# Squaring q and k one quad later in a fused attention and mixture-of-experts kernel

## The chip, the cores and the metric

The kernel runs on one core of a Trainium2 chip. The time is the device time of one execution in microseconds (us). Each run is classed fast or slow (slow for a single core: over 1.5% above the fastest run of the same kernel), and ratios use fast runs alone. PE is TensorE, ACT ScalarE, DVE VectorE, POOL GpSimd, SP the queue that issues most transfers. L189 is line 189 of the kernel.

## The reference

Attention over 8 batches and 12 heads (448 tokens, head size 64) with RMS-normalised q and k, then a soft mixture of 8 experts with 32 slots.

```python
q_n, k_n = rmsnorm(q, g_q), rmsnorm(k, g_k)         # x / sqrt(mean(x*x) + 1e-6) * g
attn = softmax(q_n @ k_n.T / 8)
x = (attn @ v) as [3584, 768]
logits = x @ phi                                    # 768 x 32
slot_input = softmax_over_tokens(logits).T @ x
slot_out[e] = relu(slot_input[e] @ w1[e]) @ w2[e]   # 8 experts, 768x1024 and 1024x768
out = softmax_over_slots(logits) @ slot_out
```

## The kernel before

A *quad* is four heads; there are 24 quads, three per batch. Iteration Q of the loop computes scores, exponentials and products of quad Q, in seven score steps, and prepares later quads between them. The preparation of one quad is: load q and k (f32, 448 KB each), square them (ACT for q, POOL for k), sum the squares (DVE), two activations for the reciprocal root (ACT), scale to bf16 (POOL), transpose (PE), copy out (DVE). v is loaded by four transfers and copied to bf16 on POOL. Every third iteration (4, 7, 10, ...) also carries the expert work of one batch: `moe_logits` after step 1 and `moe_sin` after step 5; its last products spill into the iteration behind it. The expert weights (16 of 1.5 MB in bf16, cast by the transfer from f32) are loaded by POOL during the loop, three of them by way of a copy in DRAM.

```python
place("raw", 2 * 2 * 2 * NT * D, 3)     # q and k as loaded: three quads
place("sq", 2 * 2 * 2 * NT * D, 1)      # their squares: one
place("qkn", 2 * NT * 128, 2)           # scaled q and k: two
place("vraw", 2 * 2 * NT * D, 2)
# ...
for Q in range(NQ + 2):
    # load(Q + 4): q and k, on the SP queue       (special cases for Q == 0 left out)
    # score(Q, 0); square(Q + 3, 0) on ACT; square(Q + 3, 1) on POOL; products of Q - 1
    # score(Q, 1); rowsum(Q + 3, 0)
    # score(Q, 2); trans(Q + 1, 0); evac(Q + 1, 0); scaleqk(Q + 2, 0)
    # score(Q, 3); norm(Q - 1, 1); trans(Q + 1, 1); vcopy(Q + 1); scaleqk(Q + 2, 1); loadv(Q + 3)
    # score(Q, 4); ov(Q, 0, 0, 4); evac(Q + 1, 1)
    # score(Q, 5); ov(Q, 0, 4, 7); rowsum(Q + 3, 1)
    # score(Q, 6); norm(Q, 0); rsqrt(Q + 3); loads of expert weights
```

Each engine, and the SP queue, works through its instructions in this order. `norm` (DVE) frees the PSUM that the next `ov` (PE) writes.

The softmax here doesn't subtract the row's maximum and nothing guards it: scores larger than these inputs give would overflow.

## Time and profile before

| | before |
|---|---|
| median of the first three runs | 331.62 us (328.18 to 333.1) |
| span of the profiled run | 329.2 us |
| first exponential of iteration 1 / of iteration 21 | 30.1 / 239.2 us |
| after the last exponential | 67.4 us |
| ACT, POOL, PE, DVE busy | 59, 50, 71, 58% |

The start of an iteration is read from the first of its seven exponentials (L252 on ACT). An iteration without any stall takes 7.62 us here; the mean is 10.46.

### The profile page before, as it was taken

How to read it: one execution, taken by the hardware profiler on the slowest of the kernel's cores; microseconds unless marked ns; L12 is line 12 of the kernel's file. 1: busy time of each engine (PE TensorE's matmuls, PEld its weight loads, DVE VectorE, ACT ScalarE, POOL GpSimd, SP SyncE). 2: the span in 40 equal slices, each digit the busy share in tenths (PEclk: the TensorE clock that was granted, in tenths of full speed). 3: DMA queues.
4: the chain of work that ended last, by engine and by line, in shares of the span. 5: the costliest groups of instructions: out<-in, count | busy, mean ns of one | idle time of the engine just before them, and what ended most of it. 6: DMA issues, size and time to landing. Idle time of an engine off the chain costs nothing.

```text
span 329.2 us, 8387 instructions
## 1 busy us (share of the span) xinstructions
PE 234.6 (71%) x3564; PEld 167.0 (51%) x3564; DVE 192.0 (58%) x315; ACT 193.6 (59%) x268; POOL 164.4 (50%) x187
## 2 busy tenths in 40 slices
PE   8465988578878675719788576847688768889910
PEld 3233666356556454417565354635465558874400
DVE  5644787578686485726977485745756551126820
ACT  4385897579767683737787576753797600006710
POOL 0375987659497295619688196637693000000000
PEclk9757899699998799987999799789799975555555
DMA  6967999996979939994999959999999997006996
GB/s 214 244 157 229 226 258 265 243 257 144 257 218 208 279 75 246 238 288 114 239 252 187 249 147 242 242 261 263 216 188 207 212 370 271 4 4 249 401 415 277
DMA packets 45350, 74.53 MB, mean 226 GB/s; under 512 B 3968, under 2 KB 36736, under 8 KB 44928
## 3 DMA queue, kind: packets, MB, share of 16 engines
q1 hardware_dynamic: 29616, 48.77, 47.1%
q0 software_dynamic: 15376, 25.22, 43.2%
q8 instruction: 28, 0.46, 0.6%
q14 instruction: 10, 0.08, 0.1%
q10 hardware_dynamic: 320, 0.00, 0.1%
HBM read 88.18 MB, written 15.73 MB: 316 GB/s over the span
## 4 chain that ended last, share of the span: by engine, by line
DMA 31%; PE 30%; DVE 11%; ACT 10%; POOL 8%; issue 4%; SPq 2%; ACTq 0%; POOLq 0%
DMA arena<-in_q_dram 22%; PE ov L265 7%; PE sc L251 7%; ACT arena L252 6%; DMA arena<-in_k_dram 6%; POOL arena L207 4%; DVE eT L319 3%; PE hTp L472 3%; PE soTp L481 3%; PE op L511 3%; DVE arena L276 3%; PE qkTp L225 2%; ACT arena L189 2%; DMA g<-in_g_q_dram 2%; POOL arena L187 2%
## 5 line engine op out<-in xcount | busy, mean ns | idle before, releaser
L252 ACT ACTIVATE arena<-sc 128x896 bf16<-128x896 f32 x168 | 147.4, 914 | 31.8 <-PE sc L251 31.1
L251 PE MATMUL sc<-arena 128*128 128x448 bf16 x336 | 101.6, 388 | 39.1 <-ACT arena L252 38.4
L265 PEld LDWEIGHTS <-arena 128*128 128x128 bf16 x1344 | 64.9, 104 | 63.3 <-DVE arena L276 32.2
L265 PE MATMUL ov<-arena 128*128 128x65 bf16 (+1 forms) x1344 | 72.6, 207 | 27.8 <-DVE arena L276 27.7
L195 DVE TENSOR_REDUCE ss<-arena 128x14 f32<-128x896 f32 x48 | 52.0, 1085 | 67.7 <-ACT arena L189 59.9
L207 POOL TENSOR_TENSOR arena<-arena,rs 128x896 bf16<-128x896 f32 x47 | 80.5, 1713 | 13.1 <-ACT rs L200 6.9
L187 POOL TENSOR_TENSOR arena<-arena 128x896 f32<-128x896 f32 x21 | 35.3, 1682 | 67.4 <-DMA arena<-in_k_dram 27.5
L251 PEld LDWEIGHTS <-arena 128*128 128x128 bf16 x336 | 26.7, 104 | 43.7 <-issue 41.7
L189 ACT ACTIVATE arena<-arena 128x896 f32<-128x896 f32 x27 | 25.5, 945 | 37.3 <-DMA arena<-in_q_dram 35.3
L225 PE MATMUL qkTp<-ident,arena 128*128 128x128 bf16 x360 | 32.6, 241 | 2.2 <-DVE arena L207 1.1
L276 DVE TENSOR_TENSOR arena<-ov,rd 128x512 bf16<-128x512 f32 x48 | 33.2, 691 | 1.7
L515 ACT ACTIVATE wown<-op,arena 128x768 f32<-128x768 f32 x14 | 12.4, 899 | 35.9 <-PE op L512 35.9
L225 PEld LDWEIGHTS <-arena 128*128 128x128 bf16 x360 | 26.2, 109 | 9.7 <-POOL arena L207 3.2
L236 DVE COPY arena<-qkTp 64x896 bf16<-64x896 bf16 x48 | 29.6, 617 | 1.3 <-PE qkTp L225 0.4
L232 DVE TENSOR_SCALAR arena<-qkTp,gg 128x896 bf16<-128x896 bf16 x24 | 16.2, 676 | 8.3 <-PE qkTp L225 8.2
L511 PE MATMUL op<-arena,eT 32*128 32x512 bf16 x28 | 16.0, 618 | 1.4 <-ACT wown L515 0.7
L517 DVE TENSOR_SCALAR wown<-op,arena 128x768 f32<-128x768 f32 x14 | 14.2, 1017 | 4.6 <-PE op L512 4.4
L290 DVE COPY arena<-xTp 128x1024 bf16<-128x1024 bf16 x24 | 16.3, 680 | 0.7 <-PE xTp L287 0.7
L287 PE MATMUL xTp<-ident,arena 128*128 128x128 bf16 x192 | 14.6, 219 | 1.4 <-DVE arena L276 1.0
L287 PEld LDWEIGHTS <-arena 128*128 128x128 bf16 x192 | 12.7, 98 | 5.9 <-DVE arena L276 1.2
L319 DVE COPY eT<-eTp 32x448 bf16<-32x448 bf16 x8 | 15.2, 1901 | 0.2
L275 DVE RECIPROCAL rd<-ov 128x8 f32<-128x8 f32 x48 | 9.9, 207 | 6.0 <-PE ov L265 5.5
(63 smaller groups left out, 195.6 us busy)
## 6 DMA issues: line engine op xcount, KB each, us to landing
wown<-in_moe_w_dram POOLq DMA_DIRECT2D x10, 1536.0 KB, 15.5
arena<-in_q_dram SPq DMA_DIRECT2D x24, 448.0 KB, 9.1
arena<-in_k_dram SPq DMA_DIRECT2D x24, 448.0 KB, 10.6
out_dram<-wown SPq DMA_DIRECT2D x12, 768.0 KB, 8.9
arena<-in_v_dram SPq DMA_DIRECT2D x48, 128.0 KB, 7.0
arena<-in_v_dram SPq DMA_DIRECT2D x48, 96.0 KB, 6.4
scr<-in_moe_w_dram POOLq DMA_DIRECT2D x3, 1536.0 KB, 16.2
arena<-in_moe_w_dram POOLq DMA_DIRECT2D x3, 1536.0 KB, 13.2
```

Source lines behind the costliest of these rows:

```text
L187: nc.gpsimd.tensor_tensor(sq(t), r, r, op=MUL)
L189: nc.scalar.activation(out=sq(t), in_=r, func=ACTF.Square)
L195: nc.vector.reduce_sum(sss[Q][:, t], sq(t).rearrange("p (r d) -> p r d", d=D), axis=AX)
L207: (eng or nc.gpsimd).tensor_tensor(qkn(Q, t).rearrange("p s (r d) -> p s r d", r=2), raw(Q)[:, t].rearrange("p r (s d) -> p s r d", d=D), ...
L225: nc.tensor.transpose(pts[t][:, i], qkn(Q, t)[:, s], ident)
L236: nc.vector.tensor_copy(kT(Q)[r, :, hh].rearrange("p w (s c) -> p w s c", s=NT), pt[r, :, 1 - hh:8 - hh])
L251: nc.tensor.matmul(sc[:, j, :S], kT(Q)[:, w].rearrange("p h c -> p (h c)")[:, kc:kc + 128], qT(Q)[:, w], start=True, stop=True)
L252: nc.scalar.activation(out=at("attn", i).rearrange("p (h c) -> p h c", h=2), in_=sc[:, :, :S], func=ACTF.Exp, scale=0.125)
L265: nc.tensor.matmul(ovs[w][:, c, o0:o0 + n], attn(i)[:, C0[c]:C0[c] + 128], mov, start=(first and i == lo and c % 2 == 0), stop=(i in (6, 13)),
L276: nc.vector.tensor_tensor(xq(Q).rearrange("p c (h w d) -> p c h w d", h=2, w=2)[:, :, :, w], o[:, :, :, :D], rd.to_broadcast([128, 4, 2, D ...
L287: nc.tensor.transpose(xps[Q][:, i], xq(Q)[:, i % 4, i // 4 * 128:i // 4 * 128 + 128], ident)
L511: nc.tensor.matmul(op[:, 0], eTtok(j, s), so4[r, :512], start=True, stop=True, tile_position=tp)
```

## The change

The intent: square quad Q+2 in iteration Q instead of Q+3, and scale it in the second half of the same iteration. A raw buffer is then held for a shorter time, and with three of them q and k of two further quads can be under way. One buffer of scaled q and k has to do. The core of the diff (prologue, first iteration and index shifts cut):

```diff
-    place("qkn", 2 * NT * 128, 2)
+    place("qkn", 2 * NT * 128, 1)
...
+    loadw(0)
...
-            square(Q + 3, 0)
-            square(Q + 3, 1, True)
+        if ahead:
+            square(Q + 2, 0)
+            square(Q + 2, 1, True)
...
-            rowsum(Q + 3, 0)
+        if ahead:
+            rowsum(Q + 2, 0)
...
-        if Q + 2 < NQ:
-            scaleqk(Q + 2, 0)
+        if ahead:
+            rowsum(Q + 2, 1)
...
             trans(Q + 1, 1)
             vcopy(Q + 1)
-        if Q + 2 < NQ:
+        if ahead:
+            rsqrt(Q + 2)
+            scaleqk(Q + 2, 0)
             scaleqk(Q + 2, 1)
...
-        while wnext < NPRE and Q >= wnext * 9 // 5:
+        while wnext < NPRE and Q >= (wnext * 5 + 2) // 3 - 1:
             loadw(wnext)
             wnext += 1
-        if Q in (NQ - 7, NQ - 6, NQ - 5):
-            castw(2 * E - NSCR + Q - (NQ - 7))
+        if Q in (NQ - 9, NQ - 7, NQ - 5):
+            castw(2 * E - NSCR + (Q - (NQ - 9)) // 2)
```

Besides the intent, the sum over the squares of k stands ahead of `norm(Q - 1, 1)` on DVE; the weights go out at other iterations.

More of the change, by code (lines that the diff above doesn't have):

```diff
@@ L338 @@
     rsqrt(1)
-    vcopy(0)
     for t in range(2):
         scaleqk(1, t)
-    wnext = 0
+    vcopy(0)
+    loadw(0)
+    wnext = 1
     for Q in range(NQ + 2):
-        on, ahead = Q < NQ, Q + 3 < NQ
+        on, ahead = Q < NQ, Q + 2 < NQ
         moe = Q - 2 if 0 <= Q - 2 < NQ else None
         mb = moe // QB if moe is not None and moe % QB == QB - 1 else None
-        if Q + 4 < NQ or Q == 0:
-            for q4 in ((3, 4) if Q == 0 else (Q + 4,)):
-                if q4 == 3 or Q > 0:
-                    load(q4, 0)
-                    load(q4, 1)
+        for q4 in (3, 4) if Q == 0 else (Q + 4,):
+            if q4 < NQ:
+                load(q4, 0)
+                load(q4, 1)
         if on:
             score(Q, 0)
-        if Q == 0:
-            square(2, 0)
-            rowsum(2, 0)
-        elif ahead:
-            square(Q + 3, 0)
-            square(Q + 3, 1, True)
+        if ahead:
+            square(Q + 2, 0)
+            square(Q + 2, 1, True)
         if 0 <= Q - 1 < NQ:
@@ L370 @@
             ov(Q - 1, 1, 10, 12)
-        if Q == 0:
-            square(2, 1)
-            rowsum(2, 1)
-            rsqrt(2)
-        elif ahead:
-            rowsum(Q + 3, 0)
+        if ahead:
+            rowsum(Q + 2, 0)
         if mb is not None:
@@ L396 @@
             vcopy(Q + 1)
-        if Q + 2 < NQ:
+        if ahead:
+            rsqrt(Q + 2)
+            scaleqk(Q + 2, 0)
             scaleqk(Q + 2, 1)
-        if Q + 3 < NQ:
-            loadv(Q + 3) if Q else (loadv(2), loadv(3))
+        for q3 in (2, 3) if Q == 0 else (Q + 3,):
+            if q3 < NQ:
+                loadv(q3)
         if on:
@@ L406 @@
             evac(Q + 1, 1)
-        if Q == 0:
-            load(4, 0)
-            load(4, 1)
-            square(3, 0)
-            square(3, 1, True)
-            rowsum(3, 0)
         if on:
@@ L416 @@
             ov(Q, 0, 4, 7)
-        if ahead:
-            rowsum(Q + 3, 1)
         if mb is not None:
@@ L426 @@
             moe_x(Q - 1)
-        if ahead:
-            rsqrt(Q + 3)
         if Q == 1:
             nc.gpsimd.dma_start(out=phi_s, in_=moe_phi.rearrange("(dc dp) s -> dp dc s", dp=128))
-        while wnext < NPRE and Q >= wnext * 9 // 5:
+        while wnext < NPRE and Q >= (wnext * 5 + 2) // 3 - 1:
             loadw(wnext)
             wnext += 1
-        if Q in (NQ - 7, NQ - 6, NQ - 5):
-            castw(2 * E - NSCR + Q - (NQ - 7))
+        if Q in (NQ - 9, NQ - 7, NQ - 5):
+            castw(2 * E - NSCR + (Q - (NQ - 9)) // 2)
         if Q in (NQ - 4, NQ - 3, NQ - 2):
```

## The prediction

> **What bounds the kernel now.** I read the page's table of slices first. The attention loop fills slices 2 to 31 (8.2 us each); behind it come the expert layers and the output.
>
> ```profile
> ACT  4385897579767683737787576753797600006710
> POOL 0375987659497295619688196637693000000000
> DMA  6967999996979939994999959999999997006996
> ```
>
> No compute engine stays at 9 through the loop: ScalarE and GpSimd jump between 1 and 9. The DMA row is at 9 in most slices but has holes (3, 4, 5, 6, 7). So the loop alternates between waiting for transfers and leaving the transfers idle. The chain that ended last says the same:
>
> ```profile
> DMA 31%; PE 30%; DVE 11%; ACT 10%; POOL 8%; issue 4%; SPq 2%; ACTq 0%; POOLq 0%
> ```
>
> Next the list of waits, for whom ScalarE and GpSimd (the squares, L189 and L187) wait, and for whom the load queue waits:
>
> ```profile
> ACT arena L189 <- DMA arena<-in_q_dram: 35.3, 11, 6.7
> POOL arena L187 <- DMA arena<-in_k_dram: 27.5, 6, 6.7
> ```
>
> ```profile
> SPq L129 <- POOL arena L217: 134.7, 21, 10.3
> ```
>
> The squares wait 35.3 us for q in 11 places. The queue waits for GpSimd's copies of v before it issues the next v, and behind those v, in order, stand the next q and k. One case, from the chain between 47 and 61 us:
>
> ```profile
> 47.32 0.81 ACT arena L252
> 48.13 0.44 ACT arena L189
> 48.57 11.08 DMA arena<-in_q_dram
> ...
> 59.67 0.95 ACT arena L189
> 60.62 0.81 ACT arena L252
> ```
>
> q of quad 7 is issued at 48.57, 1.2 us into iteration 3 (first exponential 47.3), and is wanted as soon as the first exponential of iteration 4 is through, at about 55.7. It has 7.2 us and takes 11.08: a 3.92 us stall. Of three raw buffers one is squared now, one waits squared for its scaling, so only one load can be under way, for less than an iteration.
>
> Taking every seventh exponential as the start of an iteration, iteration 1 starts at 30.1 us, iteration 21 at 239.2: 10.46 us each. Undisturbed ones (2, 3, 6, 15) take 7.62; 21 to 23, without new q or k, take 22.5 together. The tail after the last exponential (261.7 to 329.2) is 67.5 us.
>
> **What the Trainium skill says.** "DMA: Bandwidth & Descriptors", section "Issuing engines are not separate DMA queues": transfers issued by any engine share the same 16 DMA engines and interleave. The trace agrees: in 8 us windows without expert weights, q/k/v move 170 to 206 GB/s without filling the engines (shares 0.61 and 0.73); beside a weight load, at shares of 1.10 to 1.13, they get only 118 GB/s and the weights 138. "Perfetto Trace Analysis", section "Optimization Strategy": a gap that repeats on the engine that should be saturated can mean too few buffers for the next tile. That is the pattern here, and the SBUF is given: three raw buffers stay, only their use changes. Same page, "What "DMA-bound" means": find which DMA resource binds before calling a kernel DMA-bound. I do that by the windows below.
>
> **The change part by part.**
>
> *Squares one quad later.* Iteration Q squares Q+2 instead of Q+3 and scales Q+2 in the same iteration. No instruction's work is removed: 24 times the same two squares, sums and scalings. What moves is the deadline. The buffer of q(Q+4) comes free, as before, when Q+1 is scaled near the end of iteration Q-1, but it is wanted at the start of Q+2 instead of Q+1. Its allowance grows from about 7.2 to about 7.2+7.6-1 = 14 us (the 1 us since scaling ends a little later), while the median landing is 9.1 us for q, 10.6 for k and the longest q 17.1. Most stalls of one transfer should go.
>
> *What the transfers then allow.* Not all 35 us come back, because the 16 engines have a rate. From the page:
>
> ```profile
> q1 hardware_dynamic: 29616, 48.77, 47.1%
> q0 software_dynamic: 15376, 25.22, 43.2%
> ```
>
> q0 (weights) takes 0.432*329.2/25.22 = 5.64 us of all engines per MB; q1 0.471*329.2/48.77 = 3.18, and in windows with q/k/v alone 3.4. Until iteration 21 the loop needs 24*1.376 = 33.0 MB of q/k/v and 13 weight loads of 1.573 = 20.4 MB: 33.0*3.4 + 20.4*5.64 = 227 us of share. The share saturates above 1, as two windows show (columns after the five engines: PE clock, DMA share, GB/s):
>
> ```profile
> 54.80:69.40 14.60, 10.30 (x149) 7.75 (x150) 7.58 (x12) 7.64 (x12) 10.00 (x12) 0.77 1.10 263
> 116.80:126.30 9.50, 8.01 (x149) 6.13 (x150) 8.07 (x12) 7.61 (x12) 9.20 (x14) 1.00 0.66 119
> ```
>
> At 1.13, 227/1.13 = 201 us is an estimate of the floor, so iteration 21 could not start before about 203 us; it starts at 239.2 now. The difference, 36 us, is holes such as the second window (0.66 of 1.13 in 9.5 us is 4 us lost). The floor is about (203-27)/20 = 8.8 us per iteration.
>
> *One buffer of scaled q/k.* Scaling Q+2 must now follow the transposes of Q+1 in the same iteration. They are issued after the third and fourth score; scaling comes after the fourth exponential anyway. I charge nothing.
>
> *A tighter compute cycle.* Square of k, sum, the two rsqrt activations and two scalings now lie in one chain through GpSimd: 1.68 + 1.09 + 0.6 + 2*1.71 = 6.8 us, plus some 0.2 of hand-over, plus 0.94 when a weight load is issued: 7.0 to 7.9 us. Above 7.62 in about 13 of 24 iterations by some 0.3: 4 us, largely under the transfer floor.
>
> *Start.* Iteration 0 lasts 13.6 us now, with squares of both quads 2 and 3, and ends on the sum and rsqrt of quad 3. It loses quad 3's share; loads of quads 3 and 4 are issued at about 20 instead of 27 to 29 us, the first weights at about 21 instead of 28.3, into slices where the DMA row shows 7 and 9. Iteration 1 should start near 27: 3 us gained.
>
> *Weights.* The three casts to scratch and the loads go out slightly earlier in iterations; bytes are equal. The tail should stay at 67.5 us.
>
> Sum: iteration 1 at 27; twenty iterations at 9.1 (floor 8.8 with a little lost, since compute at 7.6 to 7.9 is not far below and jitter costs) = 182; last three 22.5; tail 67.5: 299 us of span. The timed run lies 1.8 above its span (330.95 against 329.2), and I add 2 for what I overlook: 303 us.
>
> **Rivals.** (1) *The transfers are already full*: the row shows 9 nearly everywhere, and depth brings nothing but longer landings. For it: saturated windows at 1.10 and more carry the worst stalls. Against it: about 24 us of holes by share in iterations 1 to 20, and 6 more in iteration 0. If only half of the holes close: 316 us. (2) *The new chain through GpSimd binds.* For it: late k now holds up rsqrt, in order on ScalarE after the fourth exponential, and the sum on VectorE ahead of a normalisation that frees the PSUM of the next products. If it makes 9.8 us of each iteration, 20*0.7 = 14 us more than my sum: 317. (3) *Everything hides*: stalls vanish, compute at 7.9 binds and the floor is lower than estimated; 20*1.2 = 24 us less: 279. It contradicts the share count, so I give it little. (4) *The tail pays*: the last weights (three loads at 7.4 us each, from 212 GB/s alone) land late after a shorter loop. They are issued in iterations 20 to 22, as before, and wanted five expert pairs later; against it.
>
> **Range and chances.** Between half of the holes closed (316) and a perfect floor (294). Faster by over 2% means below 325; it needs only 7 of some 30 us of holes. Faster 0.95, within 2% 0.04, slower 0.01.
>
> **What would show it.** The squares' waits for q and k should fall from 35.3 and 27.5 us to under 15 each; the DMA row should lose most of its 3s to 7s, with shares of 1.05 to 1.13 through iterations 1 to 20; median landing of q and k should rise (to about 12 to 15 us) as two quads queue; iterations should even out near 9 us instead of 7.6 to 16; the tail stays within 2 us of 67.5. I am wrong if the waits fall but the iterations stay above 10 us (rival 2: rsqrt waiting for sums, GpSimd or VectorE on the chain), if holes remain in the DMA row, or if the tail grows by what the loop gains.

## The result, and the profile after

The changed kernel took 307.31 us (median of four runs, 302.56 to 308.82), the kernel before 332.36 beside it. A ratio here is the mean of one kernel's fast runs over that of the other's of the same rounds, so not quite the ratio of the medians: 0.9206, with a 95% interval of 0.898 to 0.9433. It is faster.

The profiled run took 308.82 us and is classed slow, by little (2.1% above the fastest). No fast run of this kernel was profiled. I therefore rest nothing on its iterations 15 to 18 (9.7, 11.2, 11.1, 11.0 us); the fast profile of the changed kernel with a spare buffer (e2, below) shows nothing like them and stands in for them.

The table of slices of the changed kernel (7.7 us each, busy tenths):

```profile
ACT  4357858978877896987777576777877100017600
POOL 0299795988885995987876549876850000000000
DMA  6989999999999999999999999999999982008996
```

Inside the loop the holes of the DMA row are gone. ACT stays at 5 to 9 and POOL, until it has no more quads to prepare, at 4 to 9; in the kernel before ACT fell to 3 and POOL to 1 (the prediction's "between 1 and 9" holds for POOL alone). The chain that ended last, by engine:

```profile
PE 34%; DVE 27%; DMA 15%; ACT 11%; POOL 4%; issue 3%; SPq 0%; POOLq 0%; ACTq 0%
```

Transfers fell from 31% of the chain to 15%, VectorE rose from 11 to 27%. The waits of the squares and of the load queue (who waits for whom: us in total, times, longest):

```profile
ACT arena L189 <- DMA arena<-in_q_dram: 2.2, 1, 2.2
POOL arena L187 <- DMA arena<-in_k_dram: 4.5, 3, 1.7
```

```profile
SPq L129 <- POOL arena L217: 37.1, 14, 6.3
```

The squares' waits went from 35.3 and 27.5 us to 2.2 and 4.5, the queue's wait for the copies of v from 134.7 to 37.1. The window from iteration 1 to iteration 21, kernel before, then changed (width, five engines' busy time with counts, PE clock, DMA share, GB/s):

```profile
30.00:239.20 209.20, 153.34 (x2210) 110.90 (x2211) 138.81 (x219) 146.89 (x207) 139.61 (x153) 0.90 0.99 227
```

```profile
27.90:214.70 186.80, 143.82 (x2200) 105.77 (x2199) 136.26 (x218) 146.88 (x207) 143.56 (x154) 0.95 1.11 251
```

ACT does the same 146.9 us of work in 186.8 us instead of 209.2. So 22.4 us of the gain lie in these twenty iterations (the slow iterations 15 to 18 are in them; e2's fast profile takes 181.0 us) and 2.1 in front of them (iteration 1 starts at 28.0 instead of 30.1). The last three iterations give 1.7 back (24.3 us against 22.5) and the tail 0.6 (68.0 us after the last exponential against 67.4). The sum, 22.2, is to rounding the difference of the spans, 329.2 and 307.1.

Where did a stalled iteration go? The chain through one iteration shows what took the place of the transfers. First an unstalled iteration of the kernel before, then one of the changed kernel (start, us, what; pieces under 0.2 us left out):

```profile
40.50 0.85 ACT arena L189
...
41.38 1.09 DVE ss L195
42.46 0.59 DVE arena L232
...
43.20 0.70 DVE arena L276
...
43.95 0.67 PE ov L265 x16
```

```profile
74.23 0.85 ACT arena L189
75.10 1.09 DVE ss L195
76.19 0.59 DVE arena L232
76.78 0.99 DVE ss L195
77.92 0.70 DVE arena L276
78.67 0.67 PE ov L265 x16
```

From the square of q to the first products it took 43.95 - 40.50 = 3.45 us and now takes 78.67 - 74.23 = 4.44. The new piece is the 0.99 us sum over the squares of k (the second L195), ahead of the normalisation (L276). The wait of the products for the normalisation, kernel before and changed, grew with it:

```profile
PE ov L265 <- DVE arena L276: 27.7, 34, 3.9
```

```profile
PE ov L265 <- DVE arena L276: 43.8, 30, 2.7
```

In iterations 3 to 14 the lengths repeat as 8.1, 9.3, 9.0 to 9.3 us, where the kernel before had 7.6, and 8.0 to 8.8 with expert work, between its stalls.

### The profile page after: what moved, and what is told of

The parts are those of the page before. It is cut to its first block, busy times and chain, and to the rows that moved or that the text cites. A ratio compares the mean times of both kernels' runs of the same rounds, so it can differ in the third digit from the quotient of the medians.

```text
span 307.1 us, 8426 instructions
## 1 busy us (share of the span) xinstructions
PE 225.1 (73%) x3564; PEld 162.1 (53%) x3564; DVE 190.2 (62%) x315; ACT 192.7 (63%) x267; POOL 168.9 (55%) x188
## 4 chain that ended last, share of the span: by engine, by line
PE 34%; DVE 27%; DMA 15%; ACT 11%; POOL 4%; issue 3%; SPq 0%; POOLq 0%; ACTq 0%
PE ov L265 10%; DVE ss L195 10%; DMA arena<-in_v_dram 9%; ACT arena L252 8%; PE sc L251 7%; DVE arena L276 6%; DMA arena<-in_k_dram 5%; DVE eT L319 4%; PE hTp L458 3%; PE soTp L467 3%; PE op L497 3%; ACT arena L189 2%; DVE arena L232 2%; POOL arena L187 2%; PE op L498 2%
## 5 line engine op out<-in xcount | busy, mean ns | idle before, releaser
L251 PE MATMUL sc<-arena 128*128 128x448 bf16 x336 | 96.7, 372 | 11.1 <-ACT arena L252 10.2
L265 PE MATMUL ov<-arena 128*128 128x65 bf16 (+1 forms) x1344 | 70.2, 203 | 43.8 <-DVE arena L276 43.8
L265 PEld LDWEIGHTS <-arena 128*128 128x128 bf16 x1344 | 62.1, 101 | 75.1 <-DVE arena L276 45.4
L207 POOL TENSOR_TENSOR arena<-arena,rs 128x896 bf16<-128x896 f32 x47 | 79.6, 1714 | 28.1 <-issue 11.0
L195 DVE TENSOR_REDUCE ss<-arena 128x14 f32<-128x896 f32 x48 | 51.8, 1081 | 35.5 <-ACT arena L189 27.8
L187 POOL TENSOR_TENSOR arena<-arena 128x896 f32<-128x896 f32 x22 | 37.1, 1688 | 4.8 <-DMA arena<-in_k_dram 4.5
L251 PEld LDWEIGHTS <-arena 128*128 128x128 bf16 x336 | 26.4, 101 | 15.5 <-issue 12.8
L276 DVE TENSOR_TENSOR arena<-ov,rd 128x512 bf16<-128x512 f32 x48 | 33.2, 692 | 1.7
L225 PE MATMUL qkTp<-ident,arena 128*128 128x128 bf16 x360 | 28.7, 223 | 1.5 <-DVE arena L207 0.7
L225 PEld LDWEIGHTS <-arena 128*128 128x128 bf16 x360 | 22.9, 99 | 7.8 <-POOL arena L207 2.9
L189 ACT ACTIVATE arena<-arena 128x896 f32<-128x896 f32 x26 | 24.5, 942 | 3.8 <-DMA arena<-in_q_dram 2.2
L199 ACT ACTIVATE ss<-ss,eps 128x28 f32<-128x28 f32 (+1 forms) x25 | 7.9, 316 | 19.3 <-DVE ss L195 19.3
L215 POOL CAST arena<-arena 128x384 bf16<-128x384 f32 x24 | 12.3, 512 | 13.3 <-DMA arena<-in_v_dram 8.9
L275 DVE RECIPROCAL rd<-ov 128x8 f32<-128x8 f32 x48 | 10.0, 208 | 13.3 <-PE ov L265 13.2
L287 PEld LDWEIGHTS <-arena 128*128 128x128 bf16 x192 | 13.9, 104 | 6.4 <-issue 1.8
## 6 DMA issues: line engine op xcount, KB each, us to landing
arena<-in_q_dram SPq DMA_DIRECT2D x24, 448.0 KB, 11.1
```

What stands on the lines that cost most here:

```text
L187: nc.gpsimd.tensor_tensor(sq(t), r, r, op=MUL)
L189: nc.scalar.activation(out=sq(t), in_=r, func=ACTF.Square)
L195: nc.vector.reduce_sum(sss[Q][:, t], sq(t).rearrange("p (r d) -> p r d", d=D), axis=AX)
L207: (eng or nc.gpsimd).tensor_tensor(qkn(Q, t).rearrange("p s (r d) -> p s r d", r=2), raw(Q)[:, t].rearrange("p r (s d) -> p s r d", d=D), ...
L225: nc.tensor.transpose(pts[t][:, i], qkn(Q, t)[:, s], ident)
L251: nc.tensor.matmul(sc[:, j, :S], kT(Q)[:, w].rearrange("p h c -> p (h c)")[:, kc:kc + 128], qT(Q)[:, w], start=True, stop=True)
```

## The experiments

**One quad ahead again (e1).** Theory A: the gain is the depth of loads. Rival B: it is the order on the engines, the start and the weights.

```diff
-        for q4 in (3, 4) if Q == 0 else (Q + 4,):
+        for q4 in (Q + 3,):
             if q4 < NQ:
```

> The changed kernel with the depth taken back: each iteration Q issues q and k of Q+3 instead of Q+4, so one quad is under way again, all else as changed. Theory A (the gain is the depth of loads): the squares' waits for q and k come back to 25 us or more each and the time goes to 322 to 345 us. Rival B (the gain is the new order on the engines, the shorter first iteration and the earlier weights): the time stays within 2% of the changed kernel, 302 to 313 us.

Measured: 311.88 us (308.57 to 313.59), ratio 0.937 (0.928 to 0.947). The wait for q is 2.7 us, for k 12.1. The time lies inside rival B's range, but the experiment was not as strict as it looked. For what I call the allowance I now took, from the traces, the time from the issue of q to the moment at which its square is wanted (0.9 us after the iteration's first exponential), median over quads 6 to 21: it is 8.7 us in the kernel before, 18.3 in the changed one, and 11.9 here. With three buffers the load of Q+3 need not wait for the last scaling. So it is one quad ahead, but earlier.

**Two raw buffers (e11, then e14).** The strict form: two buffers, so that a load needs the scaling of the last iteration.

```diff
-    place("raw", 2 * 2 * 2 * NT * D, 3)
+    place("raw", 2 * 2 * 2 * NT * D, 2)
+    place("pad", 2 * 2 * 2 * NT * D, 1)
...
-        for q4 in (3, 4) if Q == 0 else (Q + 4,):
+        for q4 in (Q + 3,):
```

> The changed kernel with two raw buffers (a pad keeps all other places) and the load of Q+3 in iteration Q, so that a load can be issued only when the quad two before it has been scaled near the end of the last iteration: one quad under way for less than an iteration, as in the kernel before, but with the new order on the engines. The run with one quad ahead and three buffers had not done this, since its loads went out 11.9 us (median) before they were wanted, against 8.7 in the kernel before and 18.3 in the changed one. Theory A (the allowance from issue to want is the gain): the allowance falls to 9 us or less, the waits of the squares come back to 40 us or more together, and the time goes to 322 to 345 us. Rival B (order, start and weights): 302 to 313 us.

Measured: 336.95 us and a wrong output: quad 2 was loaded over quad 0 before its use, and the weights of expert 5 overwrote quad 23. Both also stalled the kernel (the first exponential came at 25.4 instead of 15.6 us, iteration 21 took 21.0 us), so the total says nothing. The mended version moves the load of quad 2 behind the scaling of quad 0 and the pad in front of the buffers:

```diff
-    place("raw", 2 * 2 * 2 * NT * D, 2)
     place("pad", 2 * 2 * 2 * NT * D, 1)
+    place("raw", 2 * 2 * 2 * NT * D, 2)
...
-    load(2, 0)
-    load(2, 1)
     loadv(1)
...
     scaleqk(0, 1, nc.vector)
+    load(2, 0)
+    load(2, 1)
```

> The run with two raw buffers again, mended: the load of quad 2 now stands behind the scaling of quad 0, whose buffer it takes, and the pad lies in front so that the weights of expert 5 do not overwrite quad 23. Its first version gave a wrong result for these two reasons, but its iterations 1 to 20 took 194.4 us against 186.7 in the changed kernel and 209.1 in the kernel before. If that reading holds, one quad under way in the new order costs only about 8 us: 313 to 320 us with a start some us later. If theory A in its strict form holds (less than one iteration of allowance brings the old stalls back), 325 us or more.

Measured: 315.89 us (315.53 to 316.58), correct, ratio 0.955 (0.950 to 0.961). Iterations 1 to 20 take 195.1 us. With one buffer less the new order still keeps 4.5 of the 7.9% of the gain (ratios 0.955 and 0.921, the latter with its wide interval), some 15 of 26 us. Theory A in its strict form falls. Depth gives about 11 us in the new order (fast runs: mean 316.0 us here, 304.7 in the changed kernel). The allowance is 12.0 us here, not the 8.7 of the kernel before: something else in the old order had made the loads late.

**Only the queue's order (e16).** The kernel before says what: the SP queue issues in order, and q and k of the next quad stood behind four loads of v. Here nothing but the place of two issues changes (and those of quad 5 in iteration 0); squares stay three quads ahead, with three buffers, and quad Q+5 still waits for the scaling of Q+2.

```diff
-        if Q + 4 < NQ or Q == 0:
-            for q4 in ((3, 4) if Q == 0 else (Q + 4,)):
-                if q4 == 3 or Q > 0:
-                    load(q4, 0)
-                    load(q4, 1)
+        if Q == 0:
+            load(3, 0)
+            load(3, 1)
...
             scaleqk(Q + 2, 0)
+        if 0 < Q and Q + 5 < NQ:
+            load(Q + 5, 0)
...
             scaleqk(Q + 2, 1)
+        if 0 < Q and Q + 5 < NQ:
+            load(Q + 5, 1)
         if Q + 3 < NQ:
             loadv(Q + 3) if Q else (loadv(2), loadv(3))
```

> The kernel before with one thing changed: the load queue issues q and k of the next quad as soon as the scaling that frees their halves of the buffer is done, ahead of the loads of v, which wait for GpSimd's copies. Still three raw buffers, squares three quads ahead, one quad under way. Theory E (much of the loss was q and k standing in the queue behind v): the median allowance for q grows from 8.7 us to 11 or more and the time falls to 310 to 322 us. If the loss was the missing buffer alone, it stays within 2% of the kernel before (324 to 338 us).

Measured: 305.27 us (303.27 to 306.42), correct, ratio 0.922 (0.917 to 0.928). This is the whole gain of the change, without the change, and faster than the 310 to 322 us that I expected. The timeline of the kernel before, POOL and SP lines around the issue of quad 7 (start, us, engine, line, what), and below it the same place in this run:

```profile
43.00 1.72 POOL L207 TENSOR_TENSOR arena<-arena,rs 128x896 bf16<-128x896 f32 x1
...
45.87 0.61 SPq L129 DMA_DIRECT2D arena<-in_v_dram  x1
46.52 0.60 SPq L130 DMA_DIRECT2D arena<-in_v_dram  x1
47.18 0.60 SPq L129 DMA_DIRECT2D arena<-in_v_dram  x1
47.87 0.59 SPq L130 DMA_DIRECT2D arena<-in_v_dram  x1
48.57 0.54 SPq L118 DMA_DIRECT2D arena<-in_q_dram  x1
```

```profile
41.62 1.72 POOL L207 TENSOR_TENSOR arena<-arena,rs 128x896 bf16<-128x896 f32 x1
...
43.37 0.37 SPq L118 DMA_DIRECT2D arena<-in_q_dram  x1
...
46.63 0.37 SPq L118 DMA_DIRECT2D arena<-in_k_dram  x1
47.06 0.60 SPq L129 DMA_DIRECT2D arena<-in_v_dram  x1
```

In the kernel before the scaling that frees the buffer of q ends at 44.72. The queue waits 1.15 us more for the copy of v, then issues v four times, 0.6 us each, until 48.46, and issues q at 48.57: 3.85 us after the buffer was free. So most of the delay is the issuing of v itself. The example is typical: over quads 6 to 23 the median is 3.87 us (1.16 of waiting, 2.70 of issuing). Here q goes out at 43.37, 0.03 us after its scaling ends, and the median is 0.03. The median allowance grows from 8.7 to 12.5 us. Theory E holds.

The changed kernel's queue shows why e14 kept so much. With the copy of v ahead of the scalings, the last v goes out while POOL still scales, and q follows 0.03 us after the scaling that frees its buffer, which ended at 72.17:

```profile
70.59 0.60 SPq L130 DMA_DIRECT2D arena<-in_v_dram  x1
72.20 0.38 SPq L118 DMA_DIRECT2D arena<-in_q_dram  x1
```

In e14 the median from the freed buffer to the issue of q is 0.14 us.

What is left in e16: iteration 1 to 21 takes 177.2 us, and iterations 13 and 21 take 15.3 and 12.9. In both POOL waits for a late v, which lands at 141.7 and 210.1 us, and the DMA shares are 1.08 and 1.14.

The Trainium skill states half of the mechanism, on "DMA: Bandwidth & Descriptors", section "Anatomy of one DMA — SWDGE (gpsimd) path": "any semaphore wait happens on the issuing sequencer before dispatch". The trace agrees, for transfers issued by SP: in the example v's 1.15 us of waiting for POOL, on the SP queue, delayed a q whose buffer was free.

**Four raw buffers in the old order (e10).** The depth by another way. Four buffers alone did not fit (the pool would need 209.8 KB per partition). Squares in bf16 and one buffer of scaled q and k make the room; the sum over bf16 squares takes 1,086 ns against 1,085 from f32, so that costs no time.

```diff
-    place("raw", 2 * 2 * 2 * NT * D, 3)
-    place("sq", 2 * 2 * 2 * NT * D, 1)
-    place("qkn", 2 * NT * 128, 2)
+    place("raw", 2 * 2 * 2 * NT * D, 4)
+    place("sq", 2 * 2 * NT * D, 1)
+    place("qkn", 2 * NT * 128, 1)
...
+        for q4 in ((3, 4) if Q == 0 else (Q + 5,)):
...
```

> The kernel before with its squares three quads ahead, but a fourth raw buffer, so that q and k of two quads are under way without any reordering; to make room the squares are written in bf16 and scaled q/k have one buffer. Theory A: the same depth by another way gives most of the gain, 300 to 315 us. Rival B: it stays at 322 us or more, because the order was what mattered. If theory C holds as well, it is faster than the changed kernel, as its plain iterations stay at 7.62 us; if rival D holds, it is within 2% of it.

Measured: 303.96 us (302.65 to 305.32), ratio 0.918 (0.911 to 0.925). Depth works too, by giving an allowance of 14.4 us, though q still goes out 6.5 us (median) after its buffer is free. Most of its iterations take 7.6, 9.0, 8.0 us, but iterations 13, 20 and 21 take 14.7, 12.3 and 10.6. The window of iteration 13:

```profile
128.70:143.40 14.70, 9.51 (x149) 7.25 (x150) 7.57 (x11) 7.65 (x12) 10.29 (x13) 0.88 1.11 260
```

The transfers are full in it (share 1.11, 260 GB/s). What the faster engines save, the transfers take back: rival D, that the transfers' rate sets the pace (its wording stands under e3).

**The same three kernels without most expert weights (e5, e6, e13).** All experts use the first expert's weights (wrong output), so 14 of 16 weight loads are left out and the engines show their own pace.

```diff
-    wt = [wview(wplace[i], i) for i in range(2 * E)]
+    wt = [wview(wplace[i % 2], i) for i in range(2 * E)]
...
     def loadw(i):
+        if i > 1:
+            return
...
     def castw(i):
+        return
```

> The kernel before with only the first expert's two weights loaded and used for all experts (wrong output on purpose): 11 of 13 weight loads leave the loop. If the transfers' rate and queueing make its stalls, all iterations fall to 7.6 (plain) to 9 us (those with expert logits or sums), waits for q and k fall under 10 us, and the last exponential ends near 215 us instead of 261.5. If a one-quad allowance of 8.7 us is too short even without weights, stalls of over 20 us remain.

> The changed kernel with the first expert's two weights alone (wrong output on purpose). It shows the engines' own pace in the new order. Theory C (engines' order sets 8.1, 9.3, 9.2 us): these lengths stay as they are in nearly all of iterations 1 to 20, and the last exponential ends near 228 us, only some 8 to 12 us earlier than with all weights (238.8). Rival D (the transfers hold it to 8.9 us): the iterations fall to 7.6 to 9 us and the end to 215 us.

> The kernel with the old order and four raw buffers, with the first expert's two weights alone (wrong output on purpose). With all weights its undisturbed iterations took 7.6, 9.0, 8.0 us, but three of 14.7, 12.3 and 10.6 us gave that back. If those are the transfers' rate (rival D), they vanish here and the last exponential ends near 212 to 216 us, before that of the changed kernel with the same light weights; if they have another cause, they stay.

Measured: before 290.12, changed 297.58, four buffers 285.06 us (two runs each). From iteration 1 to 21 they take 171.0, 177.3 and 166.1 us; the last exponential ends at 224.1, 229.8 and 218.1 us, where I expected 215, 228 and 212 to 216. With few weights the order of the ranks turns round: the kernel before is 7.5 us faster than the changed one. In the changed kernel iterations 3 to 20 keep their 8.1, 9.3, 9.0 to 9.3 us to the tenth, as theory C expected, and its squares wait 3.7 us in all for q and k. Its engines' own pace is 177.3/20 = 8.87 us. The old order's is 166.1/20 = 8.3. The kernel before keeps one stall (13.3 us, iteration 4, with the second of its two weights, issued at 41.2 us, on the way). Its q still goes out 3.88 us (median) after its buffer is free, but lands 4.0 us later instead of 9.1. So with few weights the late issue costs little (171.0 against the 166.1 us with four buffers): the loss in the kernel before needs both, loads issued late and transfers slowed by the weights. In the four-buffer kernel the three long iterations vanish, as rival D expected.

**The sum behind the normalisation (e3).** `rowsum(Q + 2, 1)` of the changed kernel moves behind `norm(Q - 1, 1)`.

```diff
-        if ahead:
-            rowsum(Q + 2, 1)
...
             norm(Q - 1, 1)
+        if ahead:
+            rowsum(Q + 2, 1)
```

> The changed kernel with the sum over the squares of k issued behind the normalisation of the quad before, not ahead of it. Theory C (VectorE's order now sets the undisturbed iteration: the sum of 1.08 us stands ahead of the normalisation that frees the PSUM of the next products): the plain iterations fall from 8.11 to about 7.6 us and the first product of the second half starts 4.4 instead of 5.4 us after the first exponential; over iterations 1 to 14 some 5 to 8 us are saved, 300 us, if the transfers let it. Rival D (the transfers' rate sets the loop at about 8.9 us per iteration): single iterations change, the waits for q, k and v grow by as much, and the time stays within 1% of 307 us.

Measured: 305.75 us (304.83 to 307.52), ratio 0.923 (0.916 to 0.929): no difference is shown. The plain iterations did not fall to 7.6 but rose to 8.3; those with expert work fell from 9.3 to 8.4, and the ones behind them stayed at 9.2 to 9.4. The wait of the reciprocal root (L199) for the sum grew from 19.3 to 40.8 us: the sum now delays ACT instead of PE. My expectation of 7.6 was wrong: here the wait moved and did not go. That it must, as long as squares, sums, roots and scalings of one quad share one iteration, is argued and not shown.

**Two buffers of scaled q and k (e2).** `place("qkn", 2 * NT * 128, 2)` in the changed kernel.

> The changed kernel with two buffers of scaled q/k again. If the single buffer costs nothing, as predicted, the time is within 1.5% of the changed kernel (302 to 312 us) and no wait of the scaling (L207) for the transposes (L225) vanishes that was there. If the single buffer costs, iterations 1 to 14 get shorter than 8.1, 9.3, 9.2 us and the time falls below 300.

Measured: 305.83 us (301.54 to 308.44), ratio 0.918 (0.908 to 0.928), not to be told from the changed kernel. Its profile is of a fast run (299.8 us), and its iterations are 8.1, 9.3 and 9.0 to 9.3 us nearly throughout (two others: 10.4 and 9.7); 1 to 21 take 181.0 us.

**The weights at their old iterations (e8).** Both schedule lines of the change are undone.

```diff
-        while wnext < NPRE and Q >= (wnext * 5 + 2) // 3 - 1:
+        while wnext < NPRE and Q >= wnext * 9 // 5:
...
-        if Q in (NQ - 9, NQ - 7, NQ - 5):
-            castw(2 * E - NSCR + (Q - (NQ - 9)) // 2)
+        if Q in (NQ - 7, NQ - 6, NQ - 5):
+            castw(2 * E - NSCR + Q - (NQ - 7))
```

> The changed kernel with the expert weights loaded and cast at the iterations of the kernel before (the first one still ahead of the loop). If the new times of the weights matter, three casts in a row at iterations 17 to 19 stall the loop there and the time is 310 us or more; if not, it is within 1.5% of the changed kernel (302 to 312 us).

Measured: 302.82 us (301.85 to 304.41), ratio 0.916 (0.909 to 0.922). The new times of the weights bring nothing; the intervals overlap, so that they cost is not shown.

**Four buffers and an early start (e12).** e10 with the first weights ahead of the loop, the changed kernel's weight iterations (those lines as in the change), and quad 5 issued at the loop's start.

```diff
+    loadw(0)
+
+    wnext = 1
...
+        for q4 in ((3, 4, 5) if Q == 0 else (Q + 5,)):
```

> The kernel before with four raw buffers (squares in bf16, one buffer of scaled q/k), and in addition the first weights before the loop, the weight loads at the iterations of the changed kernel, and q and k of quad 5 issued at the loop's start. If the transfers' rate is what is left (rival D), filling the holes of the first 35 us gives 2 to 6 us over the four-buffer run: 298 to 303 us, below the changed kernel by over 1.5%. If not, it stays at 304 us.

Measured: 301.48 us (six runs, 300.72 to 301.99), ratio 0.911 (0.907 to 0.915). Its runs lie below all of e10 and of the changed kernel. It beats the kernel before by 29 us. Against the fast runs of the changed kernel (302.56 and 306.84, mean 304.7) it is 1% ahead, with overlapping intervals. Where the 2.5 us against e10 come from is open: the last exponential ends no earlier (233.0 against 232.2 us), and the tail, 66.1 against 68.6 us, varies by as much between the profiles of the other correct runs (66.6 to 68.8).

## Why the prediction was right or wrong

**The time** of 303 us with 294 to 316 held 307.31.

**The waits and holes** went as foretold: waits for q and k under 15 us each, a full DMA row, iterations of 8.1 to 9.3 us, an unchanged tail. The landing rose about as named, k into the 12 to 15 us and q to just under them. Before and changed (KB each, us to landing):

```profile
arena<-in_q_dram SPq DMA_DIRECT2D x24, 448.0 KB, 9.1
arena<-in_k_dram SPq DMA_DIRECT2D x24, 448.0 KB, 10.6
```

```profile
arena<-in_q_dram SPq DMA_DIRECT2D x24, 448.0 KB, 11.1
arena<-in_k_dram SPq DMA_DIRECT2D x24, 448.0 KB, 12.4
```

**The step that failed is the cause**: "one waits squared for its scaling, so only one load can be under way, for less than an iteration". The three buffers alone did not make the loads late. "The buffer of q(Q+4) comes free, as before, when Q+1 is scaled" was silently read as "is issued then". The issue came 3.87 us later (median), behind the loads of v. I had quoted the line of the queue waiting for the copies of v (134.7 us) and priced it at nothing; what counted was not that sum but the 1.16 us of it after the buffer was free, and the 2.70 us of issuing v. e16 shows that the queue's order alone gives 25 us, with the same three buffers; e14 shows that the new order keeps some 15 of 26 us with two. Nor is "only one load" so: in 11 of 17 cases of the kernel before the next q was issued before the last of q and k had landed (quads 6 to 22), in e16 in 16 of 17, with an allowance of 12.5 us, longer than its mean iteration of 8.9. Depth is a second way to the same end and is worth about 11 us on top of the new order. How the gain of the change itself splits between the two was not tested apart: the changed kernel with the copy of v back between the scalings was not run.

**The allowance** of 7.2 growing to 14 us was mis-sized: medians 8.7 and 18.3. Both ends were short: the example was one of the tight ones, and iterations of 9 us, not 7.6, now separate issue and want.

**The floor of the transfers**, iteration 21 not before 203 us, was not undercut by any correct run with all weights: 205.6 (e10), 206.5 (e16), 208.5 (e8), 208.8 (e2), 210.3 (e12). In e10 with few weights (e13) it falls to 195.5. For the old order with early loads the transfers are thus what holds; that the floor lies at 203 us stays an estimate.

**The compute cycle** is the mis-sized term. I put it at 7.0 to 7.9 us, "largely under the transfer floor". It measures 8.87 us (e6), just above the 8.8 that I estimated for the transfers. Two things were missing: iterations with expert work, and those behind them, take 8.0 to 9.0 us in the old order too, and the sum ahead of the normalisation adds 0.99 us to the path to the products. So that "floor 8.8 with a little lost" gave nearly the right number is in part luck, as two limits happen to lie close: in the changed kernel the engines' order accounts for 177.3 of the 181.0 us that the fast profile of e2 shows. Rival 2 was half right: the new order binds, through VectorE (and, with the sum later, through ACT, as e3 shows), but at 8.9 and not 9.8 us.

**The single buffer and the tail** show no cost, as predicted, and the start at 27 came at 28.0 us.

## What to carry to other kernels

Before buying depth with buffers, look at when each load is issued against when its buffer is free. The SP queue here issued in order, so four loads of v, one of them waiting for another engine, held up a q that could have gone 3.87 us earlier. When a stall goes, compare the new pace with the engines' own pace (leave most of the transfers out) and with the transfers' rate: in the changed kernel both stood near 8.8 us an iteration, and four repairs (the change, e16, e10 and e12) all ended between 301 and 308 us.

## What the Trainium skill lacked or had wrong

- "Perfetto Trace Analysis", section "Optimization Strategy": for a gap that repeats, the passage on bubbles suggests too little room for the next tile, buffer count or tile sizes. Here such gaps largely went without another buffer: reordering the issues of one queue took 330.4 to 305.3 us. The section's general advice, to find what the wait is for and make it start sooner, covers this; the order of issues in one queue is not among the causes it names.
- "DMA: Bandwidth & Descriptors", section "Anatomy of one DMA — SWDGE (gpsimd) path", says that semaphore waits are on the issuing sequencer, but neither it nor "Issuing engines are not separate DMA queues" draws the consequence: a load that waits, or several issued in a row, delay those behind them. Here 1.16 us of waiting and 2.70 us of issuing four loads of v (medians) came before a q whose buffer was free.
